# Sliding-window attention with a top-1 mixture of experts on one core: first loads in two pieces, a later place for eight scalar operations, for each pair's loads and for the expert slots' gathers

## The chip, the cores and the metric

The kernel runs on one core of a Trainium2 chip. A core has five engines that run their own instruction streams side by side: TensorE (PE in the profile; PEld is its loading of weights), VectorE (DVE), ScalarE (ACT), GpSimd (POOL) and SyncE (SP), which issues most of the direct transfers. The metric is the device time of one execution in microseconds (us); smaller is better.

## The reference

```python
scores = scale * np.matmul(q, k.transpose(0, 1, 3, 2))      # B 4, H 8, S 768, D 64
keep = is_sink | in_window                                  # 4 sinks, window of 128
scores = np.where(keep, scores, -1000000000.0)
scores = scores - np.max(scores, axis=-1, keepdims=True)
a = np.exp(scores)
a = a / (np.sum(a, axis=-1, keepdims=True) + 1e-09)
...
x = attn_out.transpose(0, 2, 1, 3).reshape(B * S, H * D)    # 3072 x 512
logits = x @ w_gate                                         # 8 experts
e_idx = np.argmax(logits, axis=1)
...
for e in range(E):
    mask = e_idx == e
    h = np.maximum(x[mask] @ w1[e], 0.0)                    # 512 x 1024
    ye = h @ w2[e]                                          # 1024 x 512
    out[mask] = gate_w[mask, None] * eom[mask, e, None] * ye
```

Causal attention over a window of 128 keys and four sink keys gives 3072 token rows of 512. Each row goes to the one expert with the largest gate value; its output is scaled by two gate factors.

## The kernel before

**Attention.** The 32 heads are worked as 16 pairs. `pair_step(i)` runs three stages, g = 0, 1, 2, and holds three pairs at once: the scores of pair i (`score`, two tiles of 128 queries for each stage), the transposes, sinks and product with v of pair i − 1 (`trans`, `sink`, `av`, `av_sink`), and the normalising and gating of pair i − 2 (`norm`, `gate1`, `gate2`). The order of the instructions on every engine is the order in which the program writes them.

- `load(p)` (L797) fetches a pair's q (tile qr, 128x768) and k (kr, 128x792) on SP, three buffers each. At the start of `pair_step(i)` stand `load_v(i)` (L804, tile vt, 128x768, two buffers) and `load(i + 2)`.
- `scale` (L808, POOL) multiplies a pair's q by 1/8, 256 columns at a time.
- `score(p, t)`: two matmuls (L821) fill one of two score tiles s; DVE masks them (L825 for the first tile of a pair, L827 and L829 for the others), takes the maximum (L831), and ACT the exponential (L833, tile e).
- `sink(i - 1)` makes the sinks' weights hl and writes them into psk with three transfers on SP (L875); `av_sink` (L898) multiplies psk by the sinks' values at the end of the pair's product. `norm` writes the finished rows x to the scratch xd (L929).
- `small_loads` fetches, before the first pair, the number of sinks and the window (nsw_i), and calls `scalars()`, eight small DVE operations (L149 to L159) that turn these two into floats and into a flag on whether they are the 4 and 128 for which the kernel is written.
- `behind` is a list of transfers that fetch the first experts' weights (names such as a0h and a0l: h is the rounded part of a weight, l the remainder). At the end of each of the three stages of a pair, one entry is taken from it and issued on SP.

**Expert slots.** After attention the rows are sorted by expert into slots. Four early slots (`early_slots`) begin while the last pairs finish; their gathers (tile xg, index tile idx_e) are issued in the last pairs, and PE transposes the gathered rows at L579. Then `slots()` goes through thirteen slots whose sizes stand in `SIZES = (6, 6, 4, 4, 4, 4, 2, 2, 2, 1, 1, 1, 1)` in units of 64 rows. For each slot:

- `load_ids` (L744, L745, L748) fetches its row indices on SP into a column of the tile idx; it runs three slots ahead (`AHEAD = 3`).
- `rows_of` issues the gathers, one indirect transfer on POOL for each 128 rows (`gather`, L516, tile xg, three buffers).
- `x_parts` transposes the rows on PE (L534; L684 for a slot of 64 rows). The products with w1 follow: L563 and others, and for a slot of one tile (`single_parts`) L621, whose relu on DVE is hr (L602) and is transposed on PE (L608). Then come the products with w2 (L673, L694 and L710).
- `put` scales the result (L654, ACT, tile y) and writes it to the output with an indirect transfer on POOL (L655, 'DMA out_dram' in the rows). A put waits until the put before it has landed.
- The weights come as raw f32 transfers of 512 KB (L493, four buffers); ACT rounds them (L503) and DVE or POOL subtracts to get the remainder (L504).

In `single_parts` one score tile holds both halves (512 columns each) of the first product; the second half, `products(1, ...)`, writes the same tile from which the relu of the first half reads. In `slots()` the generator `parts` holds a product piece by piece; its last step writes the puts. After that step, if the next slot's rows have been transposed (`x`), the gathers of the slot after it are issued by `rows_of(queue[0])`.

Of the kernel before, what the change touches and what calls it, by code (L numbers as in the profile page):

```python
# [10 lines left out]
I32 = mybir.dt.int32  # L11
# [43 lines left out]
def moe_kernel(tc, qT, kx, vx, vs, wgo, w1, w2, nsink, window, out):  # L55
# [7 lines left out]
    with ctx:  # L63
# [97 lines left out]
        def small_loads(q):  # L161
            q.dma_start(out=wgt, in_=wgo)
            for j, src in enumerate((nsink, window)):
                q.dma_start(out=nsw_i[:, j, :], in_=src.bitcast(I32).partition_broadcast(P))
            q.dma_start(out=xd[0, 0:DM].rearrange("(p c) -> p c", p=P), in_=tab[:, 0, 0, 0:4])
            q.dma_start(out=xd[0:1, DM:XW], in_=tab[0:1, 0, 0, 0:1])
            scalars()
# [162 lines left out]
        idx = rt.tile([P, NSLOT, NT_MAX, 4], I32, name="idx")  # L330
# [280 lines left out]
        def single_parts(mp, w, xs, hs):  # L611

            (wh, wl), (xh, xl) = w, xs
            both = s_tile()

            def products(q, ds):
                qs = slice(q * 512, (q + 1) * 512)
                for d in ds:
                    wd, wld = wh[d][:, qs], wl[d][:, qs]
                    for i, (x, a) in enumerate(((xh, wd), (xh, wld), (xl, wd))):  # L620
                        nc.tensor.matmul(out=both[:, q, :], lhsT=x[:, d, 0:P], rhs=a,  # L621
                                         start=d == 0 and i == 0, stop=d == ND - 1 and i == 2)
# [13 lines left out]
            h0 = relu(mp, both[:, 0, :])  # L636
# [5 lines left out]
            h1 = relu(mp, both[:, 1, :])  # L642
# [78 lines left out]
        for q in SEQ:  # L721
            cols = [[idx[:, q, i, j:j + 1] for j in range(3)] for i in range(-(-SIZES[q] // 2))]
            plan.append((exp_i[0:1, q:q + 1], cols, SIZES[q] == 1, q))
# [12 lines left out]
        def load_ids(q):  # L736

            at = nc.sync.value_load(lin_i[0:1, q:q + 1], min_val=0, max_val=(E - 1) * NJP + NJ)
            z = SIZES[q]
            for a in range(2):  # L740
                r = slice(a * U, (a + 1) * U)
                if z == 1:
                    src = unitd[:, bass.ds(at, 1), :]
                    nc.sync.dma_start(out=idx[r, q, 0:1, 0:2], in_=src[:, :, 0:2])  # L744
                    nc.sync.dma_start(out=idx[r, q, 0:1, 2:3], in_=src[:, :, 2 + a:3 + a])  # L745
                else:
                    src = unitd[:, bass.ds(at, z), :].rearrange("u (i a) c -> u i a c", a=2)
                    nc.sync.dma_start(out=idx[r, q, 0:z // 2, 0:2], in_=src[:, :, a, 0:2])  # L748
# [13 lines left out]
        with ExitStack() as actx:  # L762
# [29 lines left out]
            def load(p):  # L792
                b, hp = divmod(p, H // 2)
                z = pt[p] = {}
                for name, src, n in (("q", qT, S), ("k", kx, KW)):
                    z[name] = qk.tile([P, n], F32, name=name + "r", bufs=3)
                    nc.sync.dma_start(out=z[name], in_=src[b, 2 * hp:2 * hp + 2].rearrange("h d s -> (h d) s"))  # L797
# [8 lines left out]
            def scale(p, g):  # L806
                q = pt[p]["q"][:, 2 * g * P:2 * (g + 1) * P]
                nc.gpsimd.tensor_scalar(out=q, in0=q, scalar1=SCALE, scalar2=None, op0=ALU.mult)  # L808
# [284 lines left out]
            def pair_step(i):  # L1093

                if have(i):
                    load_v(i)
                if have(i + 2):
                    load(i + 2)
                for g in range(3):
# [3 lines left out]
                    if g == 0:  # L1103
                        if have(i - 1):
                            trans(i - 1, 1)
                            trans(i - 1, 2)
                            sink(i - 1)
                        if have(i - 2):
                            gate1(i - 2)
# [35 lines left out]
                    if behind:  # L1145
# [85 lines left out]
            def slots():  # L1231
# [3 lines left out]
                for i, (f, k) in enumerate(steps):  # L1235
# [28 lines left out]
                    for z in tasks:  # L1264
                        next(z[1], None)
                    if f == "first" and len(xgs[k]) == 1:
# [3 lines left out]
                    if x is not None:  # L1270
                        assert next(x, None) is None
                        queue.pop(0)
                        rows_of(queue[0])
# [212 lines left out]
```

## Time and profile before

| | |
|---|---|
| median of three runs | 582.18 us (578.35 to 582.23) |
| the profiled execution | 580.31 us |
| its span, first to last instruction | 578.5 us |
| mean granted TensorE clock | 0.969 of full speed |
| PE busy | 513.3 us (89%) |
| DVE, ACT, POOL busy | 330.5, 269.5, 257.9 us |
| bytes moved by DMA | 112.83 MB |

A row of a timeline has the start, the duration (of a group, from its first start to its last end), the engine, the line, the operation with output and inputs, how many were grouped, and in square brackets the idle time of the engine before it with what ended it. In the table of waits, 'A <- B: t, n, m' says that A's line waited t us for B in n waits, the longest of m. A row of windows has the stretch, its length, the busy time of PE, PEld, DVE, ACT and POOL (with the number of instructions in brackets), the granted PE clock, the busy share of the DMA engines, and GB/s.

### The profile page before, as it was taken

The numbers are of one execution on the slowest core, as the hardware profiler recorded it, in microseconds if no ns is written. First come the engines' busy times: TensorE is split into PE (matmuls) and PEld (weight loads), VectorE is DVE, ScalarE is ACT, GpSimd is POOL, SyncE is SP. The second block draws the span as 40 slices with busy tenths as digits, with TensorE's granted clock in tenths as the row PEclk, the third lists the DMA queues.
The fourth block names the chain that finished last, engine by engine and source line by source line (L and its number), as shares of the span: only waits on it lengthen the run. The fifth ranks groups of instructions, "written<-read, shape, count | busy, mean of one in ns | idle before, by whom it ended". The sixth has DMA issues, their size and how long they took to land. (4 is left out here: it accounts for less than half of the span.)

```text
span 578.5 us, 10477 instructions
## 1 busy us (share of the span) xinstructions
PE 513.3 (89%) x3432; PEld 390.0 (67%) x3432; DVE 330.5 (57%) x752; ACT 269.5 (47%) x721; POOL 257.9 (45%) x312
## 2 busy tenths in 40 slices
PE   3999999999979998998999999995999984799992
PEld 1566656666656753848899688984867964777971
DVE  5567698698867768994633424441644642544520
ACT  2576666666647220444534335541545442345420
POOL 4557756857856322635353313342512531513420
PEclk9999999999989998999999999998999996999997
DMA  6166775568987886337778665476586684866760
GB/s 228 61 134 187 145 151 169 142 139 213 192 247 121 205 210 205 106 113 256 229 226 312 240 195 156 139 264 246 183 291 214 226 267 178 265 224 224 253 227 19
DMA packets 72496, 112.83 MB, mean 195 GB/s; under 512 B 12044, under 2 KB 38672, under 8 KB 72434
## 3 DMA queue, kind: packets, MB, share of 16 engines
q1 hardware_dynamic: 67970, 98.16, 58.6%
q0 software_dynamic: 4464, 13.91, 6.6%
q8 instruction: 30, 0.49, 0.4%
q14 instruction: 32, 0.26, 0.2%
HBM read 98.28 MB, written 13.45 MB: 193 GB/s over the span
## 5 line engine op out<-in xcount | busy, mean ns | idle before, releaser
L833 ACT ACTIVATE e<-s,nmx 128x132 f32<-128x132 f32 x192 | 69.5, 366 | 67.2 <-DVE nmx L831 56.6
L821 PE MATMUL s<-kr,qr 64*128 64x260 f32 (+1 forms) x384 | 63.1, 430 | 16.2 <-ACT e L833 10.8
L821 PEld LDWEIGHTS s<-kr,qr 64*128 64x128 f32 x384 | 30.5, 198 | 40.2 <-ACT e L833 28.4
L544 DVE SCALAR_TENSOR_TENSOR hl<-s,hh 128x512 fp32r<-128x512 f32 (+1 forms) x32 | 24.2, 757 | 58.2 <-ACT hh L543 52.8
L655 POOL DMA_INDIRECT out_dram<-y,idx x20 | 24.4, 1219 | 59.1 <-DMA idx<-unitd 14.5
L543 ACT ACTIVATE hh<-s 128x512 fp32r<-128x512 f32 (+1 forms) x32 | 20.9, 652 | 61.7 <-PE s L563 56.5
L831 DVE TENSOR_REDUCE nmx<-s 128x2 f32<-128x264 f32 x96 | 41.5, 432 | 3.3
L537 DVE TENSOR_TENSOR xl<-tp,xh 128x512 fp32r<-128x512 f32 x21 | 14.4, 689 | 45.0 <-ACT xh L536 45.0
L808 POOL TENSOR_SCALAR qr<-qr 128x256 f32<-128x256 f32 x48 | 39.9, 850 | 0.4 <-DMA qr<-in_qT_dram 0.4
L85 POOL TENSOR_SCALAR_AFFINE_SELECT g<-f 128x512 f32<-128x512 f32 (+1 forms) x48 | 28.3, 589 | 21.7 <-DVE f L850 19.0
L833 ACT ACTIVATION_READ_ACCUMULATOR e<-s,nmx 128x1 f32 x192 | 37.6, 196 | 0.0
L827 DVE COPY_PREDICATED s<-maskf,s 128x256 f32<-128x256 int32 x80 | 33.7, 421 | 6.8 <-PE s L821 6.8
L844 PE MATMUL tp<-ident,e 128*128 128x128 f32 x192 | 30.2, 297 | 0.4 <-ACT f L848 0.4
L844 PEld LDWEIGHTS tp<-ident,e 128*128 128x128 f32 x192 | 22.1, 149 | 11.9 <-issue 4.7
L536 ACT CAST xh<-tp 128x512 fp32r<-128x512 f32 x21 | 12.3, 587 | 35.8 <-PE tp L534 35.8
L85 POOL TENSOR_SCALAR_AFFINE_SELECT f<-f 128x512 f32<-128x512 f32 (+1 forms) x48 | 27.0, 563 | 3.3
L655 POOL DMA_INDIRECT out_dram<-y,idx_e x8 | 10.0, 1254 | 39.0 <-ACT y L654 22.3
L534 PE MATMUL tp<-ident,xg 128*128 128x128 f32 x84 | 13.8, 291 | 14.9 <-DMA xg<-xd,idx 14.9
L516 POOL DMA_INDIRECT xg<-xd,idx x21 | 22.1, 1051 | 10.8 <-issue 5.5
L891 PE MATMUL oA<-f,vt 128*64 128x128 f32 x256 | 26.5, 285 | 0.4
L534 PEld LDWEIGHTS tp<-ident,xg 128*128 128x128 f32 x84 | 11.2, 151 | 19.0 <-issue 16.7
L848 ACT COPY f<-tp 128x512 f32<-128x512 f32 x32 | 18.6, 582 | 0.4 <-PE tp L844 0.4
(652 smaller groups left out, 1558.2 us busy)
## 6 DMA issues: line engine op xcount, KB each, us to landing
raw<-in_w_dram SPq DMA_DIRECT2D x88, 512.0 KB
kr<-in_kx_dram SPq DMA_DIRECT2D x16, 396.0 KB
qr<-in_qT_dram SPq DMA_DIRECT2D x16, 384.0 KB
vt<-in_vx_dram SPq DMA_DIRECT2D x16, 384.0 KB
xd<-x SPq DMA_DIRECT2D x16, 384.0 KB
a0h<-in_w_dram SPq DMA_DIRECT2D x4, 512.0 KB
a0l<-in_w_dram SPq DMA_DIRECT2D x4, 512.0 KB
b0h<-in_w_dram SPq DMA_DIRECT2D x3, 512.0 KB
```

The lines of the kernel that those rows point to most:

```text
L85: nc.gpsimd.affine_select(out=ap, in_=ap if src is None else src, pattern=pattern, compare_op=op, fill=fill, base=base, channel_multiplier=cm)
L516: nc.gpsimd.indirect_dma_start(out=xg, out_offset=None, in_=xd[0:n + 1, :], in_offset=bass.IndirectOffsetOnAxis(ap=ids[0], axis=0))
L534: nc.tensor.transpose(out=tp[:, d, :], in_=xg[:, d * P:(d + 1) * P], identity=ident)
L544: nc.vector.scalar_tensor_tensor(out=lo, in0=ps, scalar=0.0, in1=hi.bitcast(F32), op0=ALU.max, op1=ALU.subtract)
L655: nc.gpsimd.indirect_dma_start(out=where, out_offset=bass.IndirectOffsetOnAxis(ap=ids, axis=0), in_=y, in_offset=None, bounds_check=rows - ...
L808: nc.gpsimd.tensor_scalar(out=q, in0=q, scalar1=SCALE, scalar2=None, op0=ALU.mult)
L821: nc.tensor.matmul(out=s[:, a, o0:P + CW], lhsT=z["q"][r, t * P:(t + 1) * P], rhs=z["k"][r, k0:k0 + P + CW - o0], start=True, stop=True)
L827: nc.vector.copy_predicated(out=both[:, :, 4:CW], mask=bc(maski[:, 1, 4:CW], 1, 2), data=s[:, :, 0:P])
L831: nc.vector.tensor_reduce(out=m, in_=both, axis=AX.X, op=ALU.max, negate=True)
L833: nc.scalar.activation(out=z["e"][:, t, a, :], in_=both[:, a, :], func=AF.Exp, bias=m[:, a:a + 1], scale=1.0, accum_out=z["rs"][:, t, a:a ...
L844: nc.tensor.transpose(out=tp[:, k, :], in_=z["e"][:, 2 * j + k // 2, k % 2, 4:CW], identity=ident)
L891: nc.tensor.matmul(out=o, lhsT=v[:, kt, r], rhs=src[:, kt, a, :], start=t == kt == 0 or t == kt + 1 == 4, stop=False, skip_group_check=True)
```

## The change

Six edits:

1. The first pair's q and k are loaded in two pieces each, q at column 256 and k at column 268: first pieces of both, then the second pieces. The first scale of the first pair is done by DVE, not POOL.
2. `scalars()` is no longer called by `small_loads`, but in `pair_step(2)` at the end of the sink's work of stage 0.
3. `load_v(i)` and `load(i + 2)` move from the start of the pair to stage 0 behind `sink(i - 1)`, and so behind its three psk transfers. `behind` is served in stages 1 and 2 only.
4. The index tile idx becomes one tile for each slot.
5. `single_parts` takes two score tiles, one for each half.
6. In `slots()`, `rows_of(queue[0])` is called before the last step of `parts`.

```diff
@@ small_loads
             q.dma_start(out=xd[0:1, DM:XW], in_=tab[0:1, 0, 0, 0:1])
-            scalars()
@@
-        idx = rt.tile([P, NSLOT, NT_MAX, 4], I32, name="idx")
+        idx = [rt.tile([P, NT_MAX, 4], I32, name="idx%d" % q) for q in range(NSLOT)]
@@ single_parts
-            both = s_tile()
+            both = [s_tile()[:, 0, :] for _ in range(2)]
...
-                        nc.tensor.matmul(out=both[:, q, :], lhsT=x[:, d, 0:P], rhs=a,
+                        nc.tensor.matmul(out=both[q], lhsT=x[:, d, 0:P], rhs=a,
...
-            h0 = relu(mp, both[:, 0, :])
+            h0 = relu(mp, both[0])
...
-            h1 = relu(mp, both[:, 1, :])
+            h1 = relu(mp, both[1])
@@ load
-                for name, src, n in (("q", qT, S), ("k", kx, KW)):
+                srcs = [(name, src[b, 2 * hp:2 * hp + 2].rearrange("h d s -> (h d) s"), n, cut)
+                        for name, src, n, cut in (("q", qT, S, 2 * P), ("k", kx, KW, 2 * CW + 4))]
+                for name, _, n, _ in srcs:
                     z[name] = qk.tile([P, n], F32, name=name + "r", bufs=3)
-                    nc.sync.dma_start(out=z[name], in_=src[b, 2 * hp:2 * hp + 2].rearrange("h d s -> (h d) s"))
+                for half in range(1 if p else 2):
+                    for name, src, n, cut in srcs:
+                        c = slice(0, n) if p else (slice(0, cut), slice(cut, n))[half]
+                        nc.sync.dma_start(out=z[name][:, c], in_=src[:, c])
@@ scale
-                nc.gpsimd.tensor_scalar(out=q, in0=q, scalar1=SCALE, scalar2=None, op0=ALU.mult)
+                eng = nc.vector if p == g == 0 else nc.gpsimd
+                eng.tensor_scalar(out=q, in0=q, scalar1=SCALE, scalar2=None, op0=ALU.mult)
@@ pair_step
-                if have(i):
-                    load_v(i)
-                if have(i + 2):
-                    load(i + 2)
                 for g in range(3):
...
                             sink(i - 1)
+
+                        if have(i):
+                            load_v(i)
+                        if have(i + 2):
+                            load(i + 2)
+                        if i == 2:
+                            scalars()
...
-                    if behind:
+                    if behind and g:
                         behind.pop(0)()
@@ slots
                         next(z[1], None)
+                    if x is not None:
+                        assert next(x, None) is None
+                        queue.pop(0)
+                        rows_of(queue[0])
                     if f == "first" and len(xgs[k]) == 1:
                         rest = parts
                     else:
                         assert next(parts, None) is None
-                    if x is not None:
-                        assert next(x, None) is None
-                        queue.pop(0)
-                        rows_of(queue[0])
```

How the instructions stand on POOL in the slots, around the profile's 467 to 502 us (b0l, a3l and c5l are remainders of weights; 'DMA out_dram' is a put, 'DMA xg' a gather). Before:

```order
L504 TENSOR_TENSOR b0l<-raw,b0h 128x1024
L655 DMA out_dram<-y,idx 3072x512 x2
L516 DMA xg<-xd,idx 128x513 x2
L504 TENSOR_TENSOR a3l<-raw,a3h 128x1024
L655 DMA out_dram<-y,idx 3072x512
L516 DMA xg<-xd,idx 128x513 x3
L504 TENSOR_TENSOR c5l<-raw,c5h 128x1024
```

and with the change (helper lines are one lower there):

```order
L503 TENSOR_TENSOR b0l<-raw,b0h 128x1024
L515 DMA xg<-xd,idx_141 128x513 x2
L654 DMA out_dram<-y,idx_140 3072x512 x2
L503 TENSOR_TENSOR a3l<-raw,a3h 128x1024
L515 DMA xg<-xd,idx_148 128x513
L654 DMA out_dram<-y,idx_144 3072x512
L515 DMA xg<-xd,idx_142 128x513 x2
L503 TENSOR_TENSOR c5l<-raw,c5h 128x1024
```

The two gathers of the first slot now stand ahead of the two puts; in the next group the gather of the slot of 64 rows is ahead of the put, and the two of the slot after it stay behind.

SP in the later pairs, around 142 to 158 us (den is a small write of gate values, the ISA rows are register work for the weights' addresses). Before:

```order
L875 DMA psk_167<-hl 8x5x128 x3
L480 ISA
L480 DMA a0l<-in_w_dram 128x1024
L929 DMA xd<-x 128x6x128
L480 ISA
L480 DMA a1h<-in_w_dram 128x1024
L480 ISA
L480 DMA a1l<-in_w_dram 128x1024
L804 DMA vt<-in_vx_dram 128x6x128
L797 DMA qr<-in_qT_dram 128x768
L797 DMA kr<-in_kx_dram 128x792
L875 DMA psk_163<-hl 8x5x128 x3
```

and with the change:

```order
L880 DMA psk_179<-hl 8x5x128 x3
L808 DMA vt<-in_vx_dram 128x6x128
L801 DMA qr<-in_qT_dram 128x768
L801 DMA kr<-in_kx_dram 128x792
L934 DMA xd<-x 128x6x128
L479 ISA
L479 DMA a0l<-in_w_dram 128x1024
L479 ISA
L479 DMA a1h<-in_w_dram 128x1024
L880 DMA psk_175<-hl 8x5x128 x3
```

Between two pairs' psk transfers there stand two weights, not three, and the next pair's v, q and k follow psk where they came ahead of it.

DVE at the start, between the first score tile and the second. Before:

```order
L825 COPY_PREDICATED s<-maskf,none 128x2x132
L831 TENSOR_REDUCE nmx<-s 128x2
L149 CAST nswf<-nsw_i 128x4
L152 TENSOR_SCALAR nswn<-nswf 128x1 x2
L153 TENSOR_SCALAR nswn<-nswf 128x2
L157 TENSOR_SCALAR nswg<-nswf 128x2
L154 TENSOR_REDUCE special<-nswn 128x1
L158 TENSOR_TENSOR nswg<-nswg,nswf 128x2
L155 CAST special_i<-special 128x1
L827 COPY_PREDICATED s<-maskf,s 128x2x128
```

and with the change:

```order
L770 MEMSET vst_180 64x512
L813 TENSOR_SCALAR qr<-qr 128x256
L92 MEMSET maskf 128x4
L113 COPY pg<-iog 128x24
L830 COPY_PREDICATED s<-maskf,none 128x2x132
L836 TENSOR_REDUCE nmx<-s 128x2
L832 COPY_PREDICATED s<-maskf,s 128x2x128
```

The scalars' operations are gone from between the first maximum and the second tile's mask, and the first scale of q has come in ahead of the first tile's mask.

More of the change, by code (lines that the diff above doesn't have):

```diff
@@ L721, in moe_kernel @@
         for q in SEQ:
-            cols = [[idx[:, q, i, j:j + 1] for j in range(3)] for i in range(-(-SIZES[q] // 2))]
+            cols = [[idx[q][:, i, j:j + 1] for j in range(3)] for i in range(-(-SIZES[q] // 2))]
             plan.append((exp_i[0:1, q:q + 1], cols, SIZES[q] == 1, q))
@@ L743, in load_ids @@
                     src = unitd[:, bass.ds(at, 1), :]
-                    nc.sync.dma_start(out=idx[r, q, 0:1, 0:2], in_=src[:, :, 0:2])
-                    nc.sync.dma_start(out=idx[r, q, 0:1, 2:3], in_=src[:, :, 2 + a:3 + a])
+                    nc.sync.dma_start(out=idx[q][r, 0:1, 0:2], in_=src[:, :, 0:2])
+                    nc.sync.dma_start(out=idx[q][r, 0:1, 2:3], in_=src[:, :, 2 + a:3 + a])
                 else:
                     src = unitd[:, bass.ds(at, z), :].rearrange("u (i a) c -> u i a c", a=2)
-                    nc.sync.dma_start(out=idx[r, q, 0:z // 2, 0:2], in_=src[:, :, a, 0:2])
+                    nc.sync.dma_start(out=idx[q][r, 0:z // 2, 0:2], in_=src[:, :, a, 0:2])
         mctx = ctx.enter_context(ExitStack())
```

## The prediction

> **What bounds the kernel now.** I read the page's head first, then TensorE's table of waits, then its timeline at the long waits, and only then the engine or queue that ends each.
>
> ```profile
> span 578.5 us, 10477 instructions
> PE 513.3 (89%) x3432; PEld 390.0 (67%) x3432; DVE 330.5 (57%) x752; ACT 269.5 (47%) x721; POOL 257.9 (45%) x312
> ```
>
> TensorE (PE) is busy for 89% of the span, every other engine for under 60%. The end is set by PE's work, by its idle time, and by the stretches in which it works at a lower clock. Idle time is 578.5 − 513.3 = 65 us. The table of waits (columns: total, times, longest) says what ends it:
>
> ```profile
> PE tp L534 <- DMA xg<-xd,idx: 14.9, 2, 8.9
> PE s L821 <- ACT e L833: 10.8, 19, 3.8
> PE tp L684 <- DMA xg<-xd,idx: 5.6, 3, 3.6
> ...
> PE oA L898 <- DMA psk<-hl: 4.3, 3, 3.6
> ...
> PE s L621 <- DVE hr L602: 3.0, 3, 1.5
> ```
>
> The gathers of token rows (xg) cost 14.9 + 5.6 = 20.5 us in five waits. The single long wait of 3.8 for ACT, the sinks' weights (psk, 4.3) and hr (3.0) are the other places that the change touches. Where they stand on PE (start, duration, operation, idle time before it and what ended that):
>
> ```profile
> 12.81 2.10 PE L821 MATMUL s<-kr,qr 64*128 64x260 f32 x8 [3.82 <-ACT e L833]
> ...
> 162.89 0.41 PE L898 MATMUL oA<-psk,vst 64*128 64x384 f32 x1 [3.57 <-DMA psk<-hl]
> ...
> 401.79 1.09 PE L534 MATMUL tp<-ident,xg 128*128 128x128 f32 x4 [5.99 <-DMA xg<-xd,idx]
> ...
> 484.71 1.08 PE L534 MATMUL tp<-ident,xg 128*128 128x128 f32 x4 [8.87 <-DMA xg<-xd,idx]
> ...
> 505.07 0.46 PE L684 MATMUL tp<-ident,xg 64*128 64x64 f32 x4 [3.57 <-DMA xg<-xd,idx]
> ```
>
> **The change part by part.** The sum is made against the profiled execution, 580.31 us with its span of 578.5. It lies 1.9 below the median of the three runs (582.18) and inside their spread.
>
> *(a) The scalars move to the third pair; the first loads come in two pieces.* DVE stood still before the second score tile's mask:
>
> ```profile
> 6.31 0.43 DVE L831 TENSOR_REDUCE nmx<-s 128x2 f32<-128x264 f32 x1
> 9.91 0.17 DVE L149 CAST nswf<-nsw_i 128x4 f32<-128x4 int32 x1 [3.17 <-DMA nsw_i<-in_window_dram]
> ...
> 10.70 0.42 DVE L827 COPY_PREDICATED s<-maskf,s 128x256 f32<-128x256 int32 x1
> ```
>
> The first row ends at 6.74, and the mask operation of L827, which needs only scores, starts at 10.70, because the eight scalar operations written ahead of it wait for a small load. Moved away, the mask can start at 6.74, 3.96 earlier; ACT's exponentials and PE's scores behind it follow, and PE's wait of 3.82 is the one that goes. The new halves let the first score start a little sooner, but the first scale now stands on DVE behind its memsets, so I count 0.1 for it. Term: −3.9. Bounds: −3.0, if the loads of the first pair's later halves are next to be late, and −4.2.
>
> A page of the Trainium skill speaks against the split: "DMA: Bandwidth & Descriptors", section "Bandwidth", asks for transfers of 1 MiB or more and gives each a fixed cost of about 2.0 us. If the two added transfers paid that one after the other, the estimate would be 4 us, which cancels this term and gives a sum of about 551; no row here shows such serial payment, and the number above does not use it.
>
> *(b) The loads of v, q and k go behind the sinks' weights, and fewer weights go with them.* SP's rows, where the long wait arises:
>
> ```profile
> 142.34 2.29 SPq L875 DMA_DIRECT2D psk<-hl  x3
> ...
> 147.47 1.35 SPq L804 DMA_DIRECT2D vt<-in_vx_dram  x1
> ...
> 152.56 5.51 SPq L875 DMA_DIRECT2D psk<-hl  x3
> ```
>
> The three psk transfers issued from 152.56 on are landed only at 162.89, 10.3 us after the first issue, behind vt, q and k on the same queue; three such issues take 2.29 us where SP is not held and 5.51 here. The three loads are 128 rows of 768, 768 and 792 floats, 1.19 MB. At the 340 GB/s of the busy stretch quoted further down that is 3.5 us of transfer no longer ahead of psk, about the wait of 3.57. What the loads wait for in turn: they leave later by the psk issues and what DVE needs before these, but q and k are loaded two pairs ahead and vt is used in the next pair. Of the row's 4.3 us I take 3.3, since x's write and two weights stay ahead of psk. Bounds −1.0 and −4.3; with the clock at half speed behind the long wait, −5.3.
>
> *(c) Two score tiles for the single half slot.* PE waited three times for hr, the relu of the first half, since both halves lay in one tile:
>
> ```profile
> 471.61 0.50 PE L621 MATMUL s<-a0h,xh 128*128 128x512 f32 x1 [1.46 <-DVE hr L602]
> ...
> 473.81 0.60 PE L608 MATMUL tp<-ident,hr 128*128 128x128 f32 x4
> ```
>
> With a tile of its own the second half starts at once, and the wait moves to the transpose (L608) of hr. Nine matmuls lie ahead of that, 473.81 − 471.61 = 2.2 us, more than the longest wait of 1.5, so it is covered. Term: −3.0; bounds −2.0 (other users of the two score tiles come closer) and −3.0.
>
> *(d) Gathers ahead of the puts on POOL.* POOL's rows at the three long waits:
>
> ```profile
> 388.34 1.00 POOL L655 DMA_INDIRECT out_dram<-y,idx  x1 [1.33 <-ACT y L654]
> 393.54 0.98 POOL L655 DMA_INDIRECT out_dram<-y,idx  x1 [4.20 <-DMA idx<-unitd]
> 394.83 0.99 POOL L516 DMA_INDIRECT xg<-xd,idx  x1 [0.30 <-issue]
> ...
> 470.44 1.39 POOL L655 DMA_INDIRECT out_dram<-y,idx  x1 [0.56 <-ACT y L654]
> 476.69 0.98 POOL L655 DMA_INDIRECT out_dram<-y,idx  x1 [4.86 <-DMA out_dram<-y,idx]
> 477.98 0.99 POOL L516 DMA_INDIRECT xg<-xd,idx  x1 [0.30 <-issue]
> ...
> 495.56 1.82 POOL L655 DMA_INDIRECT out_dram<-y,idx  x1 [0.17 <-issue]
> 497.69 1.83 POOL L516 DMA_INDIRECT xg<-xd,idx  x1 [0.30 <-issue]
> ```
>
> A put waits until the put before it has landed (4.86), and the gather stands behind both. Ahead of them the gather can be issued as soon as POOL is free: at 387.0 (388.34 − 1.33) instead of 394.83, at 469.9 instead of 477.98, at 495.4 instead of 497.69. How long it then takes is in the gathers' own row:
>
> ```profile
> DMA to landing us min/median/max: 3.9/5.8/7.5
> ```
>
> First place: 387.0 + 0.3 + 7.5 = 394.8 at the worst; PE needed the rows at 401.79 − 5.99 = 395.8. All 5.99 goes. Second place: PE needed them at 484.71 − 8.87 = 475.8, and comes 1.5 earlier by (c), so at 474.4; 469.9 + 0.3 + 5.8 = 476.0. A wait of 1.6 is left, and 7.3 goes; with 7.5 to landing 3.3 is left, with 3.9 nothing. Third place: needed at 501.5, landed at 495.4 + 0.3 + 5.8 = 501.5; I leave 0.3 and take 3.3 off, though 2.0 are left with the longest landing. The two smaller waits, 20.5 − 5.99 − 8.87 − 3.57 = 2.1, lie behind one put that takes 1.0 to 1.8 with its gap and go. Sum 5.99 + 7.3 + 3.3 + 2.1 = 18.7; −18.5. Bounds: −13 (longest landings, and the smaller waits half left) and −20.5. The puts leave later by two issues of 1.3; nothing on PE waits for them but the end of the program, and the splits of weights behind them on POOL are covered where PE has weights in hand.
>
> *(e) The clock behind the waits.* PE at its work after the three waits (PE busy, then PEclk, the granted clock, near the end of each row):
>
> ```profile
> 402.00:407.00 5.00, 5.00 (x19) 4.21 (x19) 1.54 (x3) 2.04 (x4) 0.00 (x0) 0.53 0.00 0
> 485.00:489.00 4.00, 4.00 (x16) 3.32 (x15) 1.12 (x2) 1.13 (x3) 0.00 (x0) 0.55 0.00 0
> 505.00:509.00 4.00, 3.92 (x21) 3.86 (x22) 0.00 (x0) 0.56 (x2) 0.00 (x0) 0.58 1.04 396
> ```
>
> The same work at full clock saves 5.00 × 0.47 + 4.00 × 0.45 + 4.00 × 0.42 = 5.8 us. Term −5.8, since all three waits fall under 2 us. Bounds: −2.0 (only the first place) and −6.5. A short wait does not always leave the clock alone:
>
> ```profile
> 220.53 0.38 PE L281 MATMUL tp<-rhs,ohrow 128*128 128x256 bf16 x2 [1.38 <-POOL rhs L276]
> 221.99 0.70 PE L281 MATMUL tp<-rhs,ohrow 128*128 128x256 bf16 x4 [1.07 <-POOL rhs L276]
> ```
> ```profile
> 222.00:226.00 4.00, 4.00 (x9) 1.95 (x9) 3.13 (x11) 0.00 (x0) 0.00 (x0) 0.57 0.36 112
> ```
>
> Two waits of 1.38 and 1.07 with 0.4 of work between them were followed by a clock of 0.57. The 1.6 left at the second place is a single wait, so I forecast it at full clock; at half clock the 1.8 of that place would be back, for 549. The Trainium skill, "TensorE: Matmul & The Clock Gate", Part 1, section "HAM oscillation — how this bites in real kernels", has the rule that only idle gaps above about 3.4 us cool the engine; by it the second place stays warm, and the rows at 220 to 226 do not fit it if each gap is taken alone.
>
> *(f) New costs.* The moved loads of the last pair and the weight held back by one pair now travel beside the first early gather:
>
> ```profile
> 181.16 1.21 POOL L516 DMA_INDIRECT xg<-xd,idx_e  x1 [0.35 <-DMA vt<-in_vx_dram]
> ```
> ```profile
> 187.38 1.09 PE L579 MATMUL tp<-ident,xg 128*128 128x128 f32 x8
> ```
>
> PE takes these rows 6.2 us after the issue, without a wait in the row, and a gather takes 3.9 to 7.5: there is no slack. Some 0.9 MB beside it are 2.6 us at 340 GB/s if all of it comes first, half of that if they share: +1.2. The scalars' eight operations take 1.3 us of DVE in the third pair (9.91 to about 11.2), most of it under PE's scores: +0.3. Term +1.5; bounds 0 and +5 (all of 2.6, all of 1.3, and 1 more for later vt). The separate idx tiles cost and bring nothing: the gathers' and puts' waits are for the same older loads in both orders.
>
> Sum: −3.9 − 3.3 − 3.0 − 18.5 − 5.8 + 1.5 = −33.0, so 580.3 − 33.0 = 547.3: forecast 547.
>
> **The rivals.** *Weights take the place of the gathers.* For it speak the transfers in the second long wait, and POOL's wait for a weight just behind it:
>
> ```profile
> 476.00:485.00 9.00, 0.29 (x2) 0.32 (x3) 0.74 (x2) 0.19 (x1) 2.94 (x3) 0.63 0.92 340
> ```
> ```profile
> 492.71 2.69 POOL L504 TENSOR_TENSOR a3l<-raw,a3h 128x1024 fp32r<-128x1024 f32 x1 [12.47 <-ACT a3h L503]
> ```
>
> While PE stood, the queues ran at 0.92 of their time and brought weights that PE used afterwards. If PE needs these 8.9 us sooner, it waits for weights at the second and third places instead: 7.3 + 3.3 and the clock's 1.8 + 1.7 come back, 547.3 + 14.1 = 561. Against it: no PE wait in the table of waits names a weight, and over the span the queues are far from full in the stretches around. Chance 0.20.
>
> *The gathers don't come earlier,* the change not doing what it says: the row at 393.54 names idx, the index load, as what ended its 4.20 of idle time, and if the gathers need that same load, nothing moves. Then (d) and (e) stay away: 547.3 + 18.5 + 5.8 = 572. Against it: the index loads run three slots ahead of their gathers. Chance 0.07.
>
> *The loads behind psk become late,* the one case on the other side. v, q and k are issued after a wait for the sinks' results in each of 16 pairs; first psk issues stand 10.2 us apart (142.34 and 152.56), and one transfer took 10.3 to land. It decides when vt, issued some 6 us later in its pair, lands after its use in the next: then every pair loses the excess. From 33.0 / 16 = 2.1 us a pair the gain is eaten; at 2.5 us a pair the time is 547.3 + 40 = 587. Against it: the 10.3 is met only where weights crowd the queue, and most pairs carry none. Chance 0.03, with 0.04 more for milder losses of this sort that end within 1% of before.
>
> **How the numbers follow.** The forecast has 0.66, the weights 0.20, gathers not earlier 0.07, loads late 0.03, milder losses 0.04. The likeliest case alone runs from 541 (all lower bounds: 4.2 + 5.3 + 3.0 + 20.5 + 6.5 = 39.5) to 556. The range reaches up to the weights' case with its own spread: 541 to 564. A measurement here tells about 1% (6 us) from no change. Faster by more than that: 0.66 + 0.20 + 0.07, less 0.01 for ends of these cases, 0.92; within 1% 0.05; slower 0.03.
>
> **What would show it.** In the profile of the changed kernel: no wait above 1.5 us on PE between 8 and 16 us; no psk wait above 1.5; no hr wait on L621's successor; gathers on POOL ahead of puts, with xg waits of at most 4 us in all; a granted clock of 0.9 or more behind them. I am wrong if the waits reappear under a weight's name near 470 to 510, if PE waits for vt or kr in most pairs, or if xg's waits stay at 15 or more.

## The result and the profile after

The changed kernel takes 556.2 us (median of 4 runs, 551.58 to 560.03) against 580.26 us before (4 runs, 576.67 to 582.23). The ratio is 0.9565 with a 95% interval of 0.9475 to 0.9656: faster by 3.4 to 5.3%. The ratio leaves out executions that are over 1.5% above the fastest of their kernel (here the one of 560.03), as all ratios below do; medians and ranges have them in. The forecast was 547 in a range of 541 to 564. The direction, the range and most of the mechanisms hold; the gain is 24 us where 33 were forecast. The profiled execution took 556.54 us, its span is 554.8, so 23.7 us shorter than the span before.

The head of the page after:

```profile
span 554.8 us, 10483 instructions
PE 509.0 (92%) x3432; PEld 386.8 (70%) x3432; DVE 332.4 (60%) x753; ACT 269.3 (49%) x721; POOL 261.3 (47%) x311
```

PE's busy time fell by 4.3 us. The matmuls are the same, and PE ran less of them at half clock, as the windows further down show, so I put that down to the clock. Its idle time fell from 65.2 to 45.8 us, 19.4. Together that is the 23.7. Where the idle time went, and what took its place, in PE's table of waits after (helper lines are one lower, those of the pairs five higher than before):

```profile
PE s L826 <- ACT e L838: 8.9, 19, 1.7
PE s L826 <- DVE maskf L92: 4.7, 1, 4.7
...
PE tp L578 <- DMA xg<-xd,idx_e: 3.4, 2, 2.2
PE tp L683 <- DMA xg<-xd,idx: 2.8, 2, 1.7
PE oA L903 <- DMA psk<-hl: 2.8, 1, 2.8
PE tp L533 <- DMA xg<-xd,idx: 1.7, 2, 1.3
```

Gathers in the slots: 14.9 + 5.6 = 20.5 became 1.7 + 2.8 = 4.5. The waits for hr at the products are gone. No row names a weight. But psk still costs 2.8 in one wait, the wait for ACT still has a long one of 1.7, and one row is new: 3.4 us for the early gather (idx_e), for which nothing waited before. On PE's timeline:

```profile
33.63 0.71 PE L826 MATMUL s<-kr,qr 64*128 64x260 f32 x4 [1.71 <-ACT e L838]
...
158.96 0.41 PE L903 MATMUL oA<-psk,vst 64*128 64x384 f32 x1 [2.77 <-DMA psk<-hl]
...
184.51 0.63 PE L578 MATMUL tp<-ident,xg 128*128 128x128 f32 x4 [1.18 <-DMA xg<-xd,idx_e]
...
187.38 0.45 PE L578 MATMUL tp<-ident,xg 128*128 128x128 f32 x1 [2.24 <-DMA xg<-xd,idx_e]
...
395.09 0.60 PE L533 MATMUL tp<-ident,xg 128*128 128x128 f32 x4
...
467.03 0.63 PE L533 MATMUL tp<-ident,xg 128*128 128x128 f32 x4 [1.31 <-DMA xg<-xd,idx]
...
484.05 0.46 PE L683 MATMUL tp<-ident,xg 64*128 64x64 f32 x4 [1.68 <-DMA xg<-xd,idx]
```

PE does the same 3432 matmuls in both kernels, so the start of one and the same matmul in both traces says how far ahead the changed kernel is there. This is the account of the 23.7 us:

| up to | before, us | after, us | ahead | step |
|---|---|---|---|---|
| the scores behind the first long wait | 12.81 | 8.55 | 4.26 | +4.3 |
| the third pair, behind the scalars' new place | 36.03 | 33.63 | 2.40 | −1.9 |
| the scores behind the long psk wait | 167.79 | 163.82 | 3.97 | +1.6 |
| first expert, behind the early gather | 191.34 | 193.14 | −1.80 | −5.8 |
| the first slot of 64 rows (gather 1.14 gone) | 325.21 | 325.88 | −0.67 | +1.1 |
| transpose behind an hr wait (1.1 of the step), the wait of 5.99 and its clock | 406.30 | 397.51 | 8.79 | +9.5 |
| first half slot's second hr wait | 471.61 | 461.59 | 10.02 | +1.2 |
| transpose behind the wait of 8.87 and its clock | 488.15 | 468.87 | 19.28 | +9.3 |
| behind the wait of 3.57 and its clock | 508.89 | 486.41 | 22.48 | +3.2 |
| end of PE's work, the third hr wait | 567.08 | 543.38 | 23.70 | +1.2 |

All that attention won, 4.0 us, and 1.8 more were lost at one place, between 184 and 193 us, where PE waits for the first early gather and then works at half clock. The whole gain that reaches the end comes from the slots.

The third pair's 1.9 us on DVE. Before, the score mask follows 0.20 us behind hl:

```profile
33.73 0.28 DVE L873 TENSOR_TENSOR hl<-oA,hl 40x128 fp32r<-40x128 f32 x1 [0.97 <-ACT hl L871]
33.93 0.41 DVE L827 COPY_PREDICATED s<-maskf,s 128x256 f32<-128x256 int32 x1
```

After, the eight scalar operations stand between the two, and the mask follows 2.24 us behind hl:

```profile
29.54 0.28 DVE L878 TENSOR_TENSOR hl<-oA,hl 40x128 fp32r<-40x128 f32 x1 [0.96 <-ACT hl L876]
29.75 0.27 DVE L149 CAST nswf<-nsw_i 128x4 f32<-128x4 int32 x1
...
31.78 0.42 DVE L832 COPY_PREDICATED s<-maskf,s 128x256 f32<-128x256 int32 x1
```

The clock behind the old long waits, and behind the new one (windows of the changed kernel; PE busy, ..., PEclk, DMA share, GB/s):

```profile
188.00:193.00 5.00, 4.33 (x12) 3.18 (x11) 0.00 (x0) 0.58 (x1) 0.00 (x0) 0.50 0.93 365
395.00:400.00 5.00, 5.00 (x30) 4.05 (x29) 3.44 (x6) 3.38 (x9) 1.00 (x1) 1.00 0.99 383
468.00:472.00 4.00, 3.63 (x21) 2.79 (x20) 2.48 (x4) 3.00 (x7) 0.79 (x1) 1.00 1.03 402
484.50:488.50 4.00, 4.00 (x31) 3.28 (x32) 0.34 (x1) 1.34 (x3) 0.00 (x0) 1.00 1.00 327
```

It is 1.00 in all three places that had 0.53 to 0.58 before, and 0.50 behind the early gather.

POOL at the second place, after:

```profile
458.85 2.40 POOL L503 TENSOR_TENSOR b0l<-raw,b0h 128x1024 fp32r<-128x1024 f32 x1 [6.34 <-ACT b0h L502]
461.40 1.80 POOL L515 DMA_INDIRECT xg<-xd,idx  x1 [0.16 <-issue]
463.51 0.97 POOL L515 DMA_INDIRECT xg<-xd,idx  x1 [0.30 <-issue]
464.78 1.02 POOL L654 DMA_INDIRECT out_dram<-y,idx  x1 [0.30 <-ACT hh L628]
471.21 1.95 POOL L654 DMA_INDIRECT out_dram<-y,idx  x1 [5.40 <-PE oA L672]
```

The gathers go out 0.16 us behind the weight's remainder, and it is now the second put, not a gather, that has 5.4 us of idle time in front of it. PE took the rows 5.6 us after the first issue (467.03 − 461.40), with 1.31 of waiting: the forecast had 1.6 there.

### The profile page after: what moved, and what is told of

Same layout as the page of the kernel before. It is cut to its first block, busy times and chain, and to the rows that moved or that the text cites. A ratio compares the mean times of both kernels' runs of the same rounds, so it can differ in the third digit from the quotient of the medians.

```text
span 554.8 us, 10483 instructions
## 1 busy us (share of the span) xinstructions
PE 509.0 (92%) x3432; PEld 386.8 (70%) x3432; DVE 332.4 (60%) x753; ACT 269.3 (49%) x721; POOL 261.3 (47%) x311
## 4 chain that ended last, share of the span: by engine, by line
PE 46%; DVE 17%; DMA 13%; issue 9%; ACT 8%; POOL 5%; POOLq 0%; ACTq 0%; DVEq 0%
PE s L562 13%; PE s L826 5%; PE oA L672 5%; ACT e L838 5%; PE oB L672 5%; DMA out_dram<-y,idx 4%; DMA xg<-xd,idx 4%; PE s L587 3%; PE oA L896 3%; DVE nmx L836 2%; DVE s L832 2%; DMA raw<-in_w_dram 2%; PE s L693 2%; PE s L672 2%; DMA xg<-xd,idx_e 1%
## 5 line engine op out<-in xcount | busy, mean ns | idle before, releaser
L515 POOL DMA_INDIRECT xg<-xd,idx x21 | 27.7, 1321 | 8.4 <-ACT xf L684 3.5
L654 POOL DMA_INDIRECT out_dram<-y,idx_e x8 | 8.6, 1070 | 34.7 <-ACT y L653 16.7
L275 POOL TENSOR_TENSOR rhs<-oh,ohj 128x512 bf16<-128x512 bf16 x8 | 11.2, 1421 | 16.2 <-DVE oh L266 16.2
L653 ACT ACTIVATE y<-oA,sc 128x512 f32<-128x512 f32 (+1 forms) x16 | 10.4, 648 | 17.4 <-issue 4.6
```

The lines of the kernel that those rows point to most:

```text
L515: nc.gpsimd.indirect_dma_start(out=xg, out_offset=None, in_=xd[0:n + 1, :], in_offset=bass.IndirectOffsetOnAxis(ap=ids[0], axis=0))
L654: nc.gpsimd.indirect_dma_start(out=where, out_offset=bass.IndirectOffsetOnAxis(ap=ids, axis=0), in_=y, in_offset=None, bounds_check=rows - ...
```

## The experiments

Eleven kernels, and the changed kernel a second time. All times are against the kernel before, run on the same chip; a ratio has its 95% interval.

**The scalars behind the last pair** (x1):

```diff
-                        if i == 2:
+                        if i == NP:
                             scalars()
```

> The changed kernel with the scalars' eight operations moved once more, from the third pair to the step behind the last pair's scores. Theory: in the third pair they stand on DVE between hl and the next score mask, where DVE sets the pace of the scores; PE then waited 0.53 and 1.71 us for the exponentials and 2.3 us were lost. Without them both waits go and PE reaches the pairs behind about 2.3 us earlier, and the end comes about 2 us earlier (near 554 where the changed kernel has 556). Rival: those waits come from the loads that were moved behind psk; then they stay, at 0.5 and 1.7, wherever the scalars are.

Measured: 552.6 us (550.33 to 555.41), ratio 0.9572 (0.9512 to 0.9632). PE's wait for ACT in its table:

```profile
PE s L826 <- ACT e L838: 7.2, 18, 1.2
```

The 1.7 is gone (the 1.2 left stands at 7.53 in both kernels), and the matmul of 33.63 starts at 31.99, 1.64 sooner. The other wait that was to go, of 0.53 us, stayed (at 29.08), so the scalars did not cause that one. The theory holds for the long wait and is a little large: 1.6 us ahead there and 1.9 from 47 us on, not 2.3. Whether the end moves by it the times alone cannot say: the intervals of this kernel and of the changed one overlap.

**One weight not beside the early gather** (x2), **no weights in the last two pairs** (x3):

```diff
-                    if behind and g:
+                    if behind and g and i != NP - 1:                    # x2
+                    if behind and g and i not in (NP - 2, NP - 1):      # x3
                         behind.pop(0)()
```

> The changed kernel with one weight (a3l, 512 KB) not issued in the last pair beside the first early gather but one step later. Theory A (that weight slows the gather): PE's two waits for the early gather, 1.2 and 2.2 us, fall to under 1 us in all, the half clock behind them goes (another 2.3 us), and the end comes 4 to 6 us earlier. Theory B (vt, x and the weights of the pair before, issued up to 10 us ahead of the gather, fill the queues): the waits fall by at most 1 us and the end moves by less than 2.

> As before, but no weight at all is issued in the last two pairs (a2l, a3h and a3l come behind the first early gather). Theory A: no more than with a3l alone, 4 to 6 us earlier than the changed kernel. Theory B: only this one takes away the waits for the early gather, 5 to 6 us earlier, where holding a3l alone gave under 2. Third: both leave the waits as they are, since the gather is slowed by v's load and x's write; then the end is the changed kernel's.

Measured: x2 550.6 us, ratio 0.9553 (0.9499 to 0.9606); x3 552.4 us, 0.9539 (0.9470 to 0.9608). x2's one wait for the early gather, where the changed kernel has 3.4 us:

```profile
PE tp L578 <- DMA xg<-xd,idx_e: 1.2, 1, 1.2
```
```profile
185.30:188.30 3.00, 3.00 (x16) 2.62 (x15) 0.00 (x0) 0.00 (x0) 0.00 (x0) 1.00 0.88 335
```

The clock (1.00) is full behind it, and the matmul of 193.14 starts 6.3 us earlier than in the changed kernel, 4.7 of it from this place. x3 waits 1.0 us there in two parts, but its clock was still 0.50 (the last section shows why). So theory A for the waits, though its "under 1 us" was not met: holding the one weight beside the gather takes most of them away, and holding two more adds 0.2 us. At the end x2, x3 and the changed kernel can't be told apart by their intervals.

**The loads ahead of psk again** (x4), two weights a pair kept:

```diff
             def pair_step(i):

+                if have(i):
+                    load_v(i)
+                if have(i + 2):
+                    load(i + 2)
                 for g in range(3):
...
-                        if have(i):
-                            load_v(i)
-                        if have(i + 2):
-                            load(i + 2)
```

> The changed kernel with v's, q's and k's loads back at the start of a pair, ahead of psk; two weights a pair stay. Theory (the loads ahead of psk made psk late): psk's waits return to 0.3, 0.4 and 3.6 us, against 2.8 in the changed kernel, so about 1.5 us are lost; the early gather has no vt beside it and loses 1 of its 3.4 us of waits. The end within 2 us of the changed kernel. Rival (vt beside the gather is what slows it): waits for the early gather and the half clock go, and the end comes 4 us earlier.

Measured: 554.6 us, ratio 0.9625 (0.9562 to 0.9689), as the changed kernel. Its PE timeline:

```profile
159.67 0.66 PE L903 MATMUL oA<-psk,vst 64*128 64x384 f32 x1 [3.36 <-DMA psk<-hl]
...
186.36 0.63 PE L578 MATMUL tp<-ident,xg 128*128 128x128 f32 x4 [1.09 <-DVE tokrev L216]
...
187.39 0.63 PE L578 MATMUL tp<-ident,xg 128*128 128x128 f32 x4 [0.41 <-DMA xg<-xd,idx_e]
```

Both theories were half right. psk is late again (3.36), which loses 1.9 us by 164 us; the early gather's waits shrink to 1.5 and its clock is full, which wins 4.3 back by 193. (The releaser DVE in the row at 186.36 is the inferred one; the gather landed 0.14 us earlier.) With v's load and the weight both beside the gather, five executions (the changed kernel twice, x1, x8, z1) had waits of 1.9 to 3.4 us and a clock of 0.50 to 0.60 behind them. Without one of the two, six kernels (x2, x3, x4 and, further down, y2, y3, y5) had waits of 0.9 to 1.5; the clock was 1.00 in five of them and 0.50 in x3. Each is one execution. So both loads have a part in the waits; taking one away brings the clock back mostly, not surely.

**Gathers ahead of the puts alone** (x6: edit 6 in the kernel before) and **two score tiles alone** (x7: edit 5 in the kernel before).

> The kernel before with one edit of the six: the gathers ahead of the puts in the slots. Theory: this edit with the clock behind its waits is nearly the whole gain. PE's waits for gathers in the slots fall from 20.5 us to about 4.5, the clock stays full behind them, and the time falls by 20 to 23 us, to about 557. Rival: part of that came from the separate index tiles or from the score tiles; then less than 18 us are gained and waits for gathers of over 8 us are left.

> The kernel before with the two score tiles of the single half slot alone. Theory: the three waits for hr (3.0 us) go, but the two longest gather waits stand behind them and grow by what was won, so the end moves by only about 1 us; the row of waits for hr at the products is gone. Rival: the 3.0 us come off the end.

Measured: x6 557.1 us (556.66 to 559.8), ratio 0.9607 (0.9538 to 0.9675), so 19 to 27 us less. x7 577.3 us (10 runs), ratio 0.9948 (0.9907 to 0.9990), so 0.6 to 5 us less. x6 has no wait for a gather above 0.9 us and a full clock behind the gathers, as its theory has it. But one wait is new:

```profile
455.40 1.04 ACT L503 CAST c5h<-raw 128x1024 fp32r<-128x1024 f32 x1 [1.11 <-DMA raw<-in_w_dram]
```
```profile
457.07 0.50 PE L621 MATMUL s<-a0h,xh 128*128 128x512 f32 x1 [2.54 <-ACT xh L536]
```

PE waited for ACT's xh, which stood behind the rounding of c5h, for whose transfer ACT had waited. With the half clock that followed, about 5 us of x6's lead were lost there. So a weight did hold up PE once, without a wait that names it; the changed kernel has no wait at this matmul, and why x6 has one was not tried. In the profiled executions x6 is 3.4 us ahead of the kernel before at the first expert, where its edit has not worked yet, and 22.8 at the end of PE's work: 19.4 from the slots. In x7 the rows of hr are gone and the two long waits are:

```profile
400.72 1.09 PE L534 MATMUL tp<-ident,xg 128*128 128x128 f32 x4 [6.65 <-DMA xg<-xd,idx]
...
483.68 1.08 PE L534 MATMUL tp<-ident,xg 128*128 128x128 f32 x4 [10.49 <-DMA xg<-xd,idx]
```

They were 5.99 and 8.87: of the 3.0 us that the tiles win, the two gathers take back 0.66 + 1.62 as long as they stand behind the puts; the third gather's wait fell from 3.57 to 2.73. Only the hr wait at 557 us has no gather behind it. By these rows the tiles need edit 6 for most of their gain; the time fits the theory's 1 us as well as the rival's 3, and these two edits were not run together without the others.

**The first loads in one piece** (x8), with the scale on POOL:

```diff
-                for half in range(1 if p else 2):
+                for half in range(1):
                     for name, src, n, cut in srcs:
-                        c = slice(0, n) if p else (slice(0, cut), slice(cut, n))[half]
+                        c = slice(0, n)
...
-                eng = nc.vector if p == g == 0 else nc.gpsimd
+                eng = nc.gpsimd
```

> The changed kernel with the first pair's q and k in one piece each and the first scale on POOL again. Theory: the first score starts at 4.9 us where the changed kernel has 4.7, and the second waits as before: 0.2 us are lost, which no time shows. Rival (the fixed cost of a transfer counts): the first score starts earlier, or the small loads land earlier, and the time falls by 1 us or more.

Measured: 557.5 us, ratio 0.9609 (0.9545 to 0.9672), the changed kernel's within the noise. The first score waits 5.1 us for k, where the changed kernel waits 4.7, by its row for DVE (maskf) and no longer for a load. The theory holds. The two added transfers at a fixed cost of 2.0 us each, by which I let the Trainium skill's page "DMA: Bandwidth & Descriptors" argue against the split, are not seen; the page gives that figure in its section "Anatomy of one DMA — SWDGE (gpsimd) path", for transfers issued on GpSimd, and these are issued on SP.

**One tile for the indices** (z1):

```diff
-        idx = [rt.tile([P, NT_MAX, 4], I32, name="idx%d" % q) for q in range(NSLOT)]
+        idx1 = rt.tile([P, NSLOT, NT_MAX, 4], I32, name="idx")
+        idx = [idx1[:, q] for q in range(NSLOT)]
```

> The changed kernel with the row indices of all slots in one tile again. Theory (the waits of gathers and puts are for the same older index loads in both): no difference, the time within 0.5% of the changed kernel's and PE's waits for gathers in the slots within 1 us of its 4.5. Rival (a put that reads the one tile holds back the next index load, and so a gather): waits for gathers grow by 3 us or more.

Measured: 560.3 us (553.71 to 562.2), ratio 0.9676 (0.9614 to 0.9739); the changed kernel on the same chip 0.9630 (0.9584 to 0.9677). Waits for the slots' gathers are 2.1 + 1.6 = 3.7 us, not more than the changed kernel's 4.5. The intervals overlap, and the ratio is 0.5% higher, at the edge of what was expected: a small cost of the one tile is not excluded, but the profile shows no wait for it.

**Weights one a pair and the scalars late** (y2), **scalars late and a3l held** (y5), and **the changed kernel again** as their base:

```diff
-                        if i == 2:
+                        if i == NP:
                             scalars()
...
-                    if behind and g:
+                    if behind and (g == 2 and i != NP - 1 or i >= NP):    # y2
+                    if behind and g and i != NP - 1:                      # y5
```

> The changed kernel with the scalars behind the last pair, and the first experts' weights spread: one a pair, none in the last, the rest behind. Theory (psk and the early gather are late because weights crowd the queues in which x and v go in small packets): PE's wait for psk, 2.8 us in the changed kernel, falls under 1, the early gather's waits under 1.2, the clock stays full from 160 to 195 us; with the 2.3 of the scalars the end comes 6 to 10 us earlier than the changed kernel's, near 548. Rival (x's own write ahead of psk, and v's load beside the gather, are enough): the waits stay at 2 and more, and only the scalars' 2 to 3 us are gained.

> The changed kernel with the scalars behind the last pair and no weight issued in the last pair. Each gained alone: 2.3 us in the third pair, and about 5 at the early gather with its clock. Theory: they add up to the early slots, 7 us there, of which 1 to 3 are given back where PE waits for DVE at the first slot's rows; end near 550, the changed kernel's time less 4 to 6. Rival (what one gains the other's place takes): not over 3 us.

> The changed kernel once more, on the same chip as the other three, as the base for them: 553 to 557 us, with the early gather's waits at 2 to 4 us, the wait for psk at 1 to 3 and PE's two waits of 0.5 and 1.7 us in the third pair.

Measured: y2 550.8 us, ratio 0.9494 (0.9429 to 0.9559). y5 551.0 us, 0.9553 (0.9508 to 0.9599). The changed kernel again 556.4 us, 0.9630 (0.9584 to 0.9677), its waits 2.6 for the early gather and 1.3 for psk, its clock behind the gather 0.50. y2's rows:

```profile
PE tp L578 <- DMA xg<-xd,idx_e: 1.0, 2, 0.6
...
PE oA L903 <- DMA psk<-hl: 0.6, 1, 0.6
```

y2's theory holds: with half the weights in the queue psk's wait is 0.6 us where the kernels with two a pair and the loads behind psk had 1.1 to 2.8, the early gather's waits are 1.0, and the clock is full from 160 to 195 us. y5's sum holds in the median (5.4 us less than the changed kernel), but the two intervals overlap a little. In the profiled executions y2 is 11.8 us ahead of the changed kernel at 250 us, but only 7.0 at the end. It lost 2.7 at 404 us, at a gather wait of 2.31 with half clock behind it, and 3.2 at the first slot's rows:

```profile
254.07 0.58 PE L562 MATMUL s<-xl,a1h 128*128 128x256 f32 x1 [3.33 <-DVE xl L536]
```
```profile
254.00:258.00 4.00, 3.93 (x20) 3.94 (x21) 1.15 (x2) 1.05 (x1) 0.00 (x0) 0.57 0.99 379
```

**The slots' table sooner** (y3: y2 and one edit more):

```diff
                 while lane_step(True):
-                    points(3)
+                    points(4)
```

> The version with the scalars behind the last pair and one weight a pair, and with four steps of the slots' table, not three, worked in for each step of the early slots. Where PE came 10 us earlier to the first slot's rows it waited 3.3 us for DVE (xl) and ran at half clock behind that. Theory: DVE is late there because it works through the table until just before; with the table done sooner that wait falls under 1 us and the half clock goes, 3 to 4 us at that place, and the end comes 2 to 4 us earlier than without. Rival (DVE is late by its two weight splits, c2l and c4l, which wait for their loads): the wait stays above 2.5.

Measured: 546.8 us (545.14 to 547.98, 6 runs), ratio 0.9466 (0.9423 to 0.9508). The wait for xl is gone and the clock behind it is full:

```profile
253.70:257.70 4.00, 4.00 (x36) 4.00 (x35) 0.35 (x2) 2.37 (x4) 1.02 (x1) 1.00 0.86 286
```

From y2 to y3 this place gives 5.1 us, of which 3.4 are paid in advance where the table's matmuls (L280) now come earlier, wait for POOL (5.3 us in place of 3.6) and run at half clock behind that; with a gather wait of 2.3 us and its clock that are smaller here, the end of PE's work is 4.4 us earlier (532.05 against 536.42). The theory holds for the wait: DVE was late there because of the table. That the end comes earlier than y2's is read from these two executions; the intervals of the two times overlap. y3 is the fastest kernel of the study, and its interval lies below that of the changed kernel on the same chip.

## Why the prediction was right in direction and 9 us too low

By its own terms, measured by the account above (sum −23.7 where −33.0 was forecast):

- **(a) −3.9 at the start: right.** The matmul of 12.81 came 4.26 sooner.
- **(b) −3.3 for psk: −1.6.** The three loads did leave psk's way, but the wait went from 3.57 only to 2.77 in the profiled execution (1.1 to 2.8 in eight executions with that order of loads and two weights a pair; 1.8 to 3.6 in the four with the loads ahead). I had priced what was ahead of psk by its bytes at 340 GB/s. In the changed kernel psk is issued from 149.43 on, and in these two stretches the queues were busy for 1.33 and 0.86 of their time and moved about half of that rate, or less:

```profile
148.00:152.00 4.00, 3.66 (x40) 2.58 (x40) 3.83 (x9) 3.06 (x14) 3.32 (x5) 1.00 1.33 141
152.00:156.00 4.00, 3.45 (x38) 2.38 (x36) 3.34 (x8) 1.94 (x11) 4.00 (x5) 1.00 0.86 174
```

  What was left are the weights: y2, with one a pair, waits 0.6.
- **(c) −3.0 for hr: right.** 1.1 + 1.2 + 1.2 at the three places. The wait did not come back at the transpose (0.3 there, as before). The rows of x7 show the condition: most of it needs (d).
- **(d) and (e), −18.5 and −5.8: −22.0 together.** The gathers' waits fell by 16.0 us: the third place kept 1.68 where I left 0.3, with a landing near the longest, and the smaller one at 411 us kept 1.1. The clock was full at all three places, the other 6 us. By x6, edit 6 alone makes 19.4 of this in spite of the 5 us lost at its new wait. The 1.31 left at the second place was followed by the full clock, as forecast. At the third place that was luck: behind 1.68 it was full here, behind 1.90 in the second profiled execution it was not.
- **(f) +1.5 of new costs: +7.7, over its own bound of +5. This is the step that failed,** in both of its parts. *The early gather:* I wrote that there is no slack and then charged 1.2. It cost 3.4 us of waits and 2.4 of half clock. The weight and v's load beside it have both a part in that: without one of them the waits were 0.9 to 1.5 in six kernels, and the clock was full in five. The clock was left out of this term: I had counted it only where waits were taken away, not where one was put in. *The scalars:* charged 0.3, cost 1.9. I put their 1.3 us under PE's scores without a row that showed DVE idle there; they took 2.0 on DVE between hl and the next mask, for which the scores wait through ACT (1.71). x1 takes it back.
- **The rivals.** Weights did not take the gathers' place in the changed kernel: no PE wait names one, though x6 shows that such a wait can stand under another engine's name. The gathers did come earlier. The loads behind psk were not late for their use: no wait names v, q or k after the first. Of the 9.3 us between 33.0 and 23.7, the new cost that the forecast itself named and made too small is 6.2, (d) and (e) are 2.3 and (b) 1.7; (a) and (c) gave 0.9 more than forecast.
- **The range and the signs.** The upper bounds of the terms add up to −16.0, so 564, not the 556 that I gave as the end of the likeliest case. Of the signs, two did not come: psk's wait was 2.77, not 1.5 at most, and the gathers' waits were 4.5 in the slots and 3.4 at the early gather, not 4 in all. The clock of 0.9 behind them came in the slots, not at the early gather.

## What to carry to other kernels

When transfers are moved, look for the transfer that arrives just in time beside them: a wait of zero in the profile before can be the tightest place of the program. A wait that is put in has to be charged with the clock behind it, as one that is taken away is credited with it. And a gain at one place is only a gain if the next engine in the chain has slack too: PE, nearly 12 us early, found DVE busy with a table, and had to be helped there too.

## What the runs showed of the hardware

*The clock fell after much shorter waits than 3.4 us, and by their sum in fixed stretches.* The clock records of the fourteen traces start between 14 and 24 us. From 25 us on, every single wait of PE from 1.85 us up (24 of them) was followed by a lower granted clock in the next 3 us, of 31 between 1.34 and 1.83 only four were (1.34, 1.54, 1.57 and 1.68), and none below 1.3. Short waits add up: in x3, waits of 0.87, 0.17 and 0.67 within three us were followed by 0.50, as those of 1.38 and 1.07 were in the kernel before. But in x7 and y2 the same 1.38 and 1.07 left the clock at 1.00. The records show what decides it. In each trace the stretches at half clock start whole multiples of 3.41 us apart, and all but the last of a trace take 3.41, 6.83 or 10.24 us. On that grid PE's two waits at 221 us fell into one stretch in the changed kernel (busy 0.96 of 3.41 us), and half clock followed; in y2 a boundary parted them (busy 1.70 and 2.67):

```profile
220.81:224.22 3.41, 0.96 (x6) 0.49 (x6) 2.22 (x2) 0.00 (x0) 3.08 (x2) 1.00 1.08 373
224.22:227.63 3.41, 3.41 (x8) 1.68 (x6) 2.67 (x9) 0.00 (x0) 0.00 (x0) 0.50 0.33 112
```
```profile
209.70:213.11 3.41, 1.70 (x6) 0.54 (x5) 3.06 (x7) 0.00 (x0) 2.39 (x2) 1.00 1.00 348
213.11:216.52 3.41, 2.67 (x10) 1.43 (x10) 1.93 (x7) 0.00 (x0) 0.69 (x1) 1.00 0.84 284
216.52:219.93 3.41, 3.41 (x16) 1.93 (x15) 3.18 (x18) 1.16 (x3) 0.00 (x0) 1.00 0.40 150
```

In the fourteen traces (without the last 10 us of each), all 37 of these stretches at full clock in which PE was idle for over 1.86 us were followed by one at half clock, 8 of the 33 with 1.34 to 1.86, and none of the 2007 with less. The rule of the Trainium skill that I weighed ("TensorE: Matmul & The Clock Gate", Part 1, "HAM oscillation — how this bites in real kernels": no idle gaps above about 3.4 us) is too generous for this kernel; to stay below 1.3 us of idle time in 3.41 us was safe. The same matmul behind its wait in two kernels, x8 with 1.85 us (at 409.05) and the changed kernel with 1.10 (at 411.20):

```profile
409.50:413.50 4.00, 4.00 (x22) 4.00 (x22) 0.00 (x0) 0.37 (x1) 0.00 (x0) 0.57 1.03 404
```
```profile
411.30:415.00 3.70, 3.70 (x30) 3.34 (x32) 0.21 (x1) 0.69 (x3) 0.00 (x0) 1.00 1.07 410
```

So a wait cut from 3.6 to 1.7 us, as at the third place, saves its clock only in some executions: 1.00 behind 1.68 in the changed kernel's profile, 0.68 behind 1.90 at the same place in its second.

*A small DVE operation stretches beside one of POOL.* In y2 one operation on a single column took 1.99 us while POOL subtracted a weight; the same operation (L435) took 0.16 in the changed kernel, and there another one (L426), which takes 0.17 in y2, took 2.35 beside the same subtraction:

```profile
245.84 2.35 POOL L503 TENSOR_TENSOR c5l<-raw,c5h 128x1024 fp32r<-128x1024 f32 x1 [5.74 <-ACT c5h L502]
```
```profile
246.23 1.99 DVE L435 TENSOR_TENSOR lc<-lc,special 128x1 f32<-128x1 f32 x1
```
```profile
255.12 2.35 POOL L503 TENSOR_TENSOR c5l<-raw,c5h 128x1024 fp32r<-128x1024 f32 x1 [3.22 <-ACT c5h L502]
```
```profile
255.14 2.35 DVE L426 TENSOR_TENSOR prc<-prc,io8n 128x8 f32<-128x8 f32 x1
```

Both end with POOL's operation. Which operations are held goes by their kind. Of the DVE operations that started while POOL subtracted a weight and over 0.4 us before its end, in all fourteen traces, all 28 small ones with two inputs in SBUF (TENSOR_TENSOR and SCALAR_TENSOR_TENSOR of 1 to 32 columns) lasted to its end, and so did 20 casts of 4 or 6 columns and 5 TENSOR_SCALAR of 8 or 32. None was held of the 134 that read a PSUM tile (xl, hl, hr), of 14 reciprocals, 8 maxima and sums, and 4 casts and TENSOR_SCALAR of one column. Why was not tried.
